# Scores by head in four 64x64 tiles, and alpha, K and Q turned by VectorE in 32x32 blocks

## The chip, the cores and the metric

The kernel runs on one core of a Trainium2 chip. The core has a matrix engine (TensorE, PE in the profile; its weight loads are listed apart, as PEld), two engines for elementwise work (VectorE, DVE, and ScalarE, ACT), a third for general work (GpSimd, POOL) and SyncE (SP), which here only issues transfers. Each engine runs its own instructions in the order in which the program gives them, and semaphores order the engines against each other. SBUF is the working memory of 128 partitions, PSUM the small memory that TensorE writes, in 8 banks of 2 KB a partition. The metric is the device time of one execution in microseconds (us), the median of several runs.

## What is computed

Two blocks follow each other. The first is a gated linear recurrence, for each of 4 batches and 8 heads over 768 steps, with states of 48x48:

```python
batch, n_heads, seq, head_dim = (4, 8, 768, 48)
for t in range(S):
    state = alpha[:, :, t, :, None] * state + np.einsum('bhd,bhe->bhde', k[:, :, t], v[:, :, t])
    y[:, :, t] = np.einsum('bhd,bhde->bhe', q[:, :, t], state)
```

Its output, as 3072 rows of 384 (8 heads x 48), goes through four experts of the second block, in f32:

```python
p = domain_probs / (domain_probs.sum(-1, keepdims=True) + 1e-09)
for e in range(E):                      # E = 4, w1: 384 x 1024, w2: 1024 x 384
    h = np.maximum(x @ w1[e], 0.0)
    out += p[:, e:e + 1] * (h @ w2[e])
```

## The kernel before, in words

**Units.** The recurrence is cut into 24 units, each one block of 128 steps of one batch, all 8 heads. `attention(u)` is a generator that emits one unit's instructions in 17 steps (numbered 0 to 16 here, by its `yield`s). Two heads share the 128 partitions: head 2p has its 48 features in rows 0 to 47 and head 2p+1 in rows 64 to 111 of pair p (rows in between are zero padding), so that a turned tensor is 128 rows x 4 pairs x 128 steps.

Steps 0, 1 and 2 bring alpha, K and Q into this form. The loaded tensors have steps on partitions (`ra`, `rk`, `rq`); `turned` (L274) turns them with four TensorE transposes into a PSUM tile, and ScalarE copies it out (AT at L288, KT at L293), or VectorE multiplies it by AT into QT (L307). Each step ends with `load(after, ...)`, which issues the load of the same tensor for a later unit into the same buffer, so that load waits until the buffer is read. `own_terms` (L296) makes the diagonal terms from `rq` and `rk` as they were loaded.

Steps 3 to 11 work through seven levels (block sizes m = 1, 2, ..., 64). For each level, `copy_q` copies the half of QT that belongs to the level to a buffer `qb`, `next_q` multiplies that half of QT by decays, and `next_k` makes the next level's KT. `copy_q` writes a block-diagonal layout: for each pair, head 2p's rows go to one column block and head 2p+1's rows to another, and the rest of `qb` stays zero (L778 sets it once). Thus one matmul of `products` (L355), with KT of a pair as weights (128 rows, 64 columns) and 64 moving columns of `qb`, gives the scores of both heads. Step 7 emits `products` of levels 0 to 3 and takes levels 0 and 1; step 8 takes 2 and 3; step 11 emits the matmuls `far` of level 6 (L410) and `products` of levels 4 and 5, and takes these. `take` is VectorE's predicated copy of scores into `near` (L365). The scores lie in PSUM tiles tagged `sc`, one bank each, two buffers, and `far` is one of them. Steps 12 and 13 copy `far` and `near` to `lat` on ScalarE (L423, L428). Then KT of the last level is turned back (`turn_keys`, L475), `result` makes the output from `lat`, V, QT and the state (`yps`, L450), and step 16 makes the new state (`sps`, L489). There TensorE uses 64-column tiles in seven units (`in_pairs`).

**Experts.** `up` (L531) makes h for one expert and a group of four units, `down` (L623) multiplies by w2 and adds up. From the second group on the operands are split into parts of fewer bits (`one` and `two` at L570, the parts of `hT` at L608, L610 and L616, with `make_dif` writing the third part). The weights are split once (`split_piece`, L228, on ScalarE and VectorE), kept in DRAM, and loaded again for each later group (L203).

**Order.** TensorE is given the experts' matmuls, and the attention steps are inserted between them: `deal` (L714) plans a due time for each step from costs per matmul, and `advance` (L763) emits a step as the planned clock passes it. The due times of neighbouring units' steps are drawn together for some pairs (`TOGETHER`), so that step 7 comes next to step 15 of the unit before and step 11 next to step 16. The order is the same in every execution. In the start, steps of units 0 and 1 are written out by hand, with `fill` matmuls that nobody reads. Nearly all loads are issued by SP, in one queue: activations (L174, L179 to L181) and weights (L203, L221, L222, L224).

Of the kernel before, what the change touches and what calls it, by code (L numbers as in the profile page):

```python
# [10 lines left out]
F32 = mybir.dt.float32  # L11
# [4 lines left out]
ALU = mybir.AluOpType  # L16
# [4 lines left out]
def kernel(  # L21
# [54 lines left out]
    HALF = P // 2  # L76
# [11 lines left out]
    ident_np = np.concatenate([np.eye(P), np.tile(np.eye(HALF), (2, 1))], 1).astype(np.float32)  # L88
# [8 lines left out]
    ident_all = const.tile([P, P + HALF], F32, name="ident")  # L97
    ident = ident_all[:, :P]
    masks = const.tile([P, 6, QUAD], U8, name="masks")
# [24 lines left out]
    early = {nm: const.tile([P, H, HD], F32, name=f"r{nm}") for nm in "akq"}  # L124
    spare = hid.tile([P, 3, 2 * NT], F32R, name="hT", bufs=NQ)
    apart = {nm: spare[:, i, :H * HD].bitcast(F32).rearrange("p (h d) -> p h d", d=HD)
             for i, nm in enumerate("akq")}
    values = [const.tile([P, H, HD], F32, name=f"rv{i}") for i in range(2)]

    blocks = [const.tile([P, NP, 2, HALF], F32, name=f"qb{i}") for i in range(4)]  # L130
    free = deque(blocks)

    def raw(u, nm):
        return values[u % 2] if nm == "v" else apart[nm] if u == 1 else early[nm]
# [32 lines left out]
    def load(u, names):  # L167
        if u >= len(units):
            return
        cb, b = units[u]  # L170
        for nm in names:
            src = srcs[nm][b, :, cb * P:(cb + 1) * P, :].rearrange("h s d -> s h d")
            if nm != "v":
                nc.sync.dma_start(out=raw(u, nm)[:, :, :D], in_=src)  # L174
                continue

            pairs = raw(u, nm).rearrange("p (a i) d -> p a i d", i=2)
            src = src.rearrange("p (a i) d -> p a i d", i=2)
# [101 lines left out]
    def attention(u):  # L280
# [7 lines left out]
        nc.scalar.copy(out=AT, in_=turned(pair(ra)))  # L288
# [3 lines left out]
        KT = keys()  # L292
        nc.scalar.copy(out=KT, in_=turned(pair(rk)))  # L293
# [13 lines left out]
        nc.vector.tensor_mul(QT, turned(pair(rq)), AT)  # L307
# [13 lines left out]
        def copy_q(li):  # L321
            m = LEVELS[li]
            qv = halves(QT, m)[:, :, :, 1, :]
            qb = free.popleft()
            qbs.append(qb)
            for i in range(2):
                rows = slice(HD * i, HD * (i + 1))
                nc.scalar.copy(out=qb[rows, :, i, :].rearrange("p a (b r) -> p a b r", r=m),  # L328
                               in_=qv[rows])
# [21 lines left out]
        def products(li, out):  # L351

            for p in range(NP):
                for s in range(2):
                    nc.tensor.matmul(  # L355
                        out[HALF * s:HALF * (s + 1), 2 * p:2 * p + 2, :],
                        lhsT=KTs[li][:, p, HALF * s:HALF * (s + 1)],
                        rhs=qbs[li][:, p, :, QUAD * s:QUAD * (s + 1)], start=True, stop=True)
            free.append(qbs[li])
# [10 lines left out]
        def scores():  # L370
            return ps.tile([P, 2, H, QUAD], F32, name="sc", tag="sc")


        for li in range(3):
# [6 lines left out]
        nc.vector.tensor_mul(near, ident_all[:, P:].unsqueeze(1).broadcast_to([P, H, HALF]),  # L381
                             dot.unsqueeze(2).broadcast_to([P, H, HALF]))
        yield
        banks = [scores() for _ in range(2)]
        for li in range(4):
            products(li, banks[li // 2][:, li % 2])
        next_q(3)
        next_k(3)
        take(0, banks[0][:, 0])
        take(1, banks[0][:, 1])  # L390
# [4 lines left out]
        take(2, banks[1][:, 0])  # L395
        take(3, banks[1][:, 1])
# [9 lines left out]
        far = ps.tile([P, NP // 2, 2, HALF], F32, name="far", tag="sc")  # L406

        for r in range(NP // 2):
            for s in range(2):
                nc.tensor.matmul(far[HALF * s:HALF * (s + 1), r],  # L410
                                 lhsT=KTs[6][:, 2 * r + s, :HALF], rhs=qbs[6][:, 2 * r + s],
                                 start=True, stop=True)
        for li in (4, 5):
            products(li, bank[:, li - 4])
        free.append(qbs[6])
        take(4, bank[:, 0])
        take(5, bank[:, 1])
        next_k(6)
        yield
        parts = lat.rearrange("p (r s i) c -> p r s i c", s=2, i=2)  # L420
        for s in range(2):
            rows = slice(HALF * s, HALF * (s + 1))
            nc.scalar.copy(out=parts[:HALF, :, s, :, HALF:], in_=far[rows])  # L423
# [12 lines left out]
        def result():  # L436
            yps = ps.tile([P, KC, P], F32, name="yps", tag="w")
            for c in range(KC):
# [9 lines left out]
                for n, (past, turn) in enumerate(turns):  # L448
                    for j, (p, i, in_v, in_st) in enumerate(turn):
# [4 lines left out]
                            rhs=QT[:, p, :] if past else lat[:, 2 * p + i, :],  # L454
# [314 lines left out]
    with tc.manual_schedule():  # L769
# [96 lines left out]
```

## Time and profile before

| | |
|---|---|
| median of 3 runs | 1053.27 us (1052.65 to 1053.30) |
| span of the profiled execution, first to last instruction | 1050.8 us |
| granted TensorE clock, mean | 1.000 |
| TensorE matmuls | 1033.8 us busy, 98%, 8554 instructions |
| TensorE weight loads | 899.2 us busy, 86% |
| VectorE | 778.3 us busy, 74% |
| ScalarE | 565.7 us busy, 54% |
| GpSimd | 37.7 us busy, 4% |
| DMA, mean of 16 engines | 69%, 251.66 MB, 158549 packets |

The span is what the profiler saw of one execution; the runs' times include 2 to 3 us around it. The busy times are sums over an engine's instructions, with overlaps counted once. A busy TensorE is not one at its peak, since its matmuls are pipelined and their ends are modelled; starts are measured. The attention of all units ends at about 836 us, and the last 200 us are experts alone.

The profile also has, for the instructions of the change (count, busy us, mean ns): TensorE's transposes of ra, rk and rq 92 each, about 14 us each; L355 2304 matmuls, 77.2 us; L410 192, 15.5 us; ScalarE's copies AT and KT (L288, L293) 24 each, 14.0 us each; VectorE's QT (L307) 24, 16.4 us, 685.

### The profile page before, as it was taken

What the parts mean: (1) busy time and instruction counts of PE and PEld (TensorE: products, weight loads), DVE (VectorE), ACT (ScalarE), POOL (GpSimd) and SP (SyncE); (2) the same over time, 40 slices, a digit from 0 to 9 for tenths busy, and PEclk for the clock granted to TensorE, in tenths of its full rate; (3) what the DMA queues carried; (4) which work ended last, traced back from release to release, by engine and by line L of the source; (5) the groups of instructions that cost most, each with busy time, mean ns of one, the idle gap of its engine ahead of it and who ended that gap; (6) DMA issues with size and microseconds to landing.
All of it is one profiled execution on the core that took longest, in us unless ns stands there. A gap on an engine that the chain in (4) does not pass through costs nothing.

```text
span 1050.8 us, 21723 instructions
## 1 busy us (share of the span) xinstructions
PE 1033.8 (98%) x8554; PEld 899.2 (86%) x8554; DVE 778.3 (74%) x1620; ACT 565.7 (54%) x1195; POOL 37.7 (4%) x81
## 2 busy tenths in 40 slices
PE   8899999999999999999999999999999999999998
PEld 8777777687787899898898998898989989898998
DVE  5588777668779868778877777987887875656565
ACT  4687876575657545447456436565474453323232
POOL 3000010000001000000000000000000000000000
PEclk9999999999999999999999999999999999999999
DMA  7596699997868949669669569577594454444531
GB/s 118 161 333 210 241 313 352 320 344 235 300 247 260 382 154 317 270 210 303 241 214 336 187 219 366 183 271 258 170 361 179 183 211 180 182 184 177 207 154 46
DMA packets 158549, 251.66 MB, mean 239 GB/s; under 512 B 120144, under 2 KB 134864, under 8 KB 135920
## 3 DMA queue, kind: packets, MB, share of 16 engines
q1 hardware_dynamic: 151984, 207.89, 58.7%
q0 software_dynamic: 6016, 42.08, 10.0%
q8 instruction: 67, 1.10, 0.4%
q10 hardware_dynamic: 448, 0.32, 0.1%
q14 instruction: 34, 0.28, 0.1%
HBM read 207.79 MB, written 42.47 MB: 238 GB/s over the span
## 4 chain that ended last, share of the span: by engine, by line
PE 85%; DVE 5%; ACT 4%; DMA 2%; issue 2%; SPq 1%; POOL 0%; ACTq 0%; DVEq 0%; POOLq 0%
PE ops L663 36%; PE one L570 23%; PE two L570 11%; PE sc L355 6%; PE yps L450 3%; PE tp L277 3%; ACT qb L328 2%; PE one L562 1%; PE sps L489 1%; DMA hT<-in_moe_w_dram 1%; PE far L410 1%; DVE hT L616 1%; DMA w<-in_moe_w_dram 1%; DVE near L365 1%; DVE QT L335 1%
## 5 line engine op out<-in xcount | busy, mean ns | idle before, releaser
L663 PE MATMUL ops<-w,hT 128*128 128x384 f32 x1872 | 342.7, 340 | 0.2 <-DVE hT L616 0.2
L663 PEld LDWEIGHTS ops<-w,hT 128*128 128x128 f32 x1872 | 322.6, 188 | 4.0 <-ACT t L581 0.6
L570 PE MATMUL one<-xT,w 128*128 128x512 f32 x960 | 251.8, 398 | 0.4 <-ACT t L581 0.4
L570 PEld LDWEIGHTS one<-xT,w 128*128 128x128 f32 x960 | 176.1, 188 | 38.3 <-ACT t L581 1.2
L581 ACT ACTIVATE t<-one 128x512 f32<-128x512 f32 (+1 forms) x192 | 106.7, 556 | 175.1 <-PE one L570 169.9
L328 ACT COPY qb<-QT 64x256 f32<-64x256 f32 x336 | 136.6, 407 | 58.2 <-DVE QT L335 30.3
L610 DVE SCALAR_TENSOR_TENSOR hT<-t,hT 128x512 fp32r<-128x512 f32 (+1 forms) x172 | 110.4, 642 | 63.3 <-ACT hT L608 62.0
L583 DVE TENSOR_TENSOR t<-t,two 128x512 f32<-128x512 f32 (+1 forms) x172 | 109.2, 635 | 53.2 <-PE two L570 32.0
L608 ACT ACTIVATE hT<-t 128x512 fp32r<-128x512 f32 (+1 forms) x172 | 101.8, 592 | 86.8 <-DVE t L583 86.2
L570 PE MATMUL two<-xT,w 128*128 128x512 f32 x480 | 136.5, 393 | 0.1
L570 PEld LDWEIGHTS two<-xT,w 128*128 128x128 f32 x480 | 90.0, 188 | 20.5 <-DVE acc L692 0.9
L663 PE MATMUL ops<-hT 128*128 128x384 f32 x288 | 100.8, 492 | 0.6 <-DMA hT<-in_moe_w_dram 0.3
L616 DVE SCALAR_TENSOR_TENSOR hT<-hT 128x512 fp32r<-128x512 f32 (+1 forms) x172 | 100.6, 634 | 0.0
L365 DVE COPY_PREDICATED near<-masks,sc 128x256 f32<-128x256 uint8 x144 | 77.0, 535 | 22.2 <-PE sc L355 19.3
L335 DVE TENSOR_TENSOR QT<-QT,dec 128x256 f32<-128x256 f32 x144 | 61.0, 423 | 38.8 <-ACT qb L328 38.3
L355 PEld LDWEIGHTS sc<-qb,KT 128*64 128x64 f32 x2304 | 72.7, 138 | 9.0 <-issue 4.4
L355 PE MATMUL sc<-qb,KT 128*64 128x64 f32 x2304 | 77.2, 223 | 2.6 <-ACT qb L328 2.6
L663 PEld LDWEIGHTS ops<-hT 128*128 128x128 f32 x288 | 52.1, 190 | 30.6 <-DMA hT<-in_moe_w_dram 1.2
L692 DVE SCALAR_TENSOR_TENSOR acc<-ops,p_all,acc 128x384 f32<-128x384 f32 x82 | 49.8, 614 | 27.2 <-PE ops L663 26.3
L347 ACT COPY KT<-KT 128x256 f32<-128x256 f32 x138 | 57.5, 417 | 5.1 <-PE sc L355 1.9
L348 DVE TENSOR_TENSOR KT<-KT,dec 128x256 f32<-128x256 f32 x144 | 60.0, 417 | 0.0
L562 PE MATMUL one<-xT,w 128*128 128x256 f32 (+1 forms) x240 | 46.7, 341 | 0.6 <-ACT xT L467 0.6
(90 smaller groups left out, 932.4 us busy)
## 6 DMA issues: line engine op xcount, KB each, us to landing
w<-kept SPq DMA_DIRECT2D x144, 1152.0 KB
kept<-w POOLq DMA_DIRECT2D x32, 1152.0 KB, 7.3
hT<-in_moe_w_dram SPq DMA_DIRECT2D x32, 384.0 KB
w<-in_moe_w_dram SPq DMA_DIRECT2D x48, 128.0 KB
ra<-in_alpha_dram SPq DMA_DIRECT2D x23, 192.0 KB
rk<-in_k_dram SPq DMA_DIRECT2D x23, 192.0 KB
rq<-in_q_dram SPq DMA_DIRECT2D x23, 192.0 KB
out_dram<-acc POOLq DMA_DIRECT2D x22, 192.0 KB, 7.0
```

The source lines that it names most:

```text
L328: nc.scalar.copy(out=qb[rows, :, i, :].rearrange("p a (b r) -> p a b r", r=m), in_=qv[rows])
L335: nc.vector.tensor_mul(qv, qv, spread(dv[:, :, :, 0], m))
L348: nc.vector.tensor_mul(new[:, :, :, 0, :], old[:, :, :, 0, :], spread(halved(decs[li])[:, :, :, 1], m))
L355: nc.tensor.matmul(out[HALF * s:HALF * (s + 1), 2 * p:2 * p + 2, :], lhsT=KTs[li][:, p, HALF * s:HALF * (s + 1)], rhs=qbs[li][:, p, :, QUA ...
L365: nc.vector.copy_predicated(near.rearrange("p a (b two r) -> p a b two r", two=2, r=m)[:, :, :, 1, :], mk.unsqueeze(1).broadcast_to([P, H, ...
L570: nc.tensor.matmul(out, lhsT=w[:, part, kc], rhs=x_part(gi, part, kc), start=(part == terms[0] and kc == 0), stop=(part == terms[-1] and k ...
L581: nc.scalar.activation(out=t, in_=one, func=ACT.Copy, scale=FINE)
L583: nc.vector.tensor_add(t, t, two)
L608: nc.scalar.activation(out=top, in_=x, func=ACT.Relu, scale=TRIM)
L610: nc.vector.scalar_tensor_tensor(out=low, in0=x, scalar=0.0, in1=top.bitcast(F32), op0=ALU.max, op1=ALU.subtract)
L616: nc.vector.scalar_tensor_tensor(out=dif, in0=top.bitcast(F32), scalar=1 / 4096.0, in1=low.bitcast(F32), op0=ALU.mult, op1=ALU.subtract)
L663: nc.tensor.matmul(sums[at], lhsT=h, rhs=w, start=(n == begins[at]), stop=(n == ends[at]))
```

## The change

1. **Loads.** Units 0 and 1 keep the old loads, now both in the spare `hT` buffer (`early[u]`). For all later units alpha, K and Q are also, or instead, loaded into `runs_of`: partition 32g+t, for quadrant g (head parity i = g // 2, and features 0 to 31 or from 32 on by g % 2), holds the four steps 4t to 4t+3 of each of the four heads of that parity, as one contiguous run of 176 elements (160 for the second kind). That is four loads a tensor. K and Q are loaded in the old form too, for `own_terms`, without padding; alpha is not.
2. **Turning.** `turn` is one VectorE transpose of 32x32 blocks over the whole tile, into AT, KT or QT in place of `turned` and the copies. The padding rows 48 to 63 then hold other steps' features instead of zeros; QT is multiplied by a column `features` (1 for rows of real features, 0 for others) along with AT.
3. **Scores by head.** `copy_q` is one ScalarE copy, and `qb` is half as large with no zeros in it. `products` and `far` make one matmul per head and column half, of 64 rows and 64 weight columns, with 32 (`far`: 64) moving columns, so that four tiles of 64x64 of the array are used. Heads are ordered by parity in `near`, `lat` and the scores.
4. **PSUM.** The scores of four levels lie in one tile of two banks, one bank for each row half, with a single buffer; `far` is a part of it.

```diff
-    ident_np = np.concatenate([np.eye(P), np.tile(np.eye(HALF), (2, 1))], 1).astype(np.float32)
+    ident_np = np.concatenate([np.eye(P), np.tile(np.eye(HALF), (2, 1)),
+                               np.arange(P)[:, None] % HD < D], 1).astype(np.float32)
...
-    early = {nm: const.tile([P, H, HD], F32, name=f"r{nm}") for nm in "akq"}
     spare = hid.tile([P, 3, 2 * NT], F32R, name="hT", bufs=NQ)
-    apart = {nm: spare[:, i, :H * HD].bitcast(F32).rearrange("p (h d) -> p h d", d=HD)
-             for i, nm in enumerate("akq")}
+    early = [{nm: spare[:, i, u * H * HD:(u + 1) * H * HD].bitcast(F32).rearrange("p (h d) -> p h d", d=HD)
+              for i, nm in enumerate("akq")} for u in range(2)]
+    rows_of = {nm: const.tile([P, H, D], F32, name=f"r{nm}") for nm in "kq"}
+    NTOK = P // QUAD
+    RUN = (NTOK - 1) * D + QUAD
+    runs_of = {nm: const.tile([P, NP, RUN], F32, name=f"s{nm}") for nm in "akq"}
...
-    blocks = [const.tile([P, NP, 2, HALF], F32, name=f"qb{i}") for i in range(4)]
+    blocks = [const.tile([P, NP, HALF], F32, name=f"qb{i}") for i in range(4)]
...
-                nc.sync.dma_start(out=raw(u, nm)[:, :, :D], in_=src)
+                for g in range(P // QUAD if u >= 2 else 0):
+                    i, tail = divmod(g, 2)
+                    off, n = (QUAD, RUN - HD // 4) if tail else (0, RUN)
+                    runs = srcs[nm][b].rearrange("(a i) s d -> i a (s d)", i=2)[
+                        i, :, cb * P * D:(cb + 1) * P * D].rearrange("a (t n) -> t a n", t=QUAD)
+                    nc.sync.dma_start(out=runs_of[nm][QUAD * g:QUAD * (g + 1), :, :n],
+                                      in_=runs[:, :, off:off + n])
+                if u < 2 or nm != "a":
+                    nc.sync.dma_start(out=raw(u, nm)[:, :, :D], in_=src)
...
-        nc.scalar.copy(out=AT, in_=turned(pair(ra)))
+        def turn(nm, out):
+            t = runs_of[nm]
+            t = bass.AP(tensor=t.tensor, offset=t.offset, ap=[list(t.ap[0]), [RUN, NP], [D, NTOK], [1, QUAD]])
+            nc.vector.transpose(out=out.rearrange("p a (t n) -> p a n t", n=NTOK), in_=t)
+        if u < 2:
+            nc.scalar.copy(out=AT, in_=turned(pair(ra)))
+        else:
+            turn("a", AT)
...
-        nc.scalar.copy(out=KT, in_=turned(pair(rk)))
+        if u < 2:
+            nc.scalar.copy(out=KT, in_=turned(pair(rk)))
+        else:
+            turn("k", KT)
...
-        nc.vector.tensor_mul(QT, turned(pair(rq)), AT)
+        if u < 2:
+            nc.vector.tensor_mul(QT, turned(pair(rq)), AT)
+        else:
+            turn("q", QT)
+            nc.vector.scalar_tensor_tensor(out=QT, in0=QT, scalar=features, in1=AT,
+                                           op0=ALU.mult, op1=ALU.mult)
...
-            for i in range(2):
-                rows = slice(HD * i, HD * (i + 1))
-                nc.scalar.copy(out=qb[rows, :, i, :].rearrange("p a (b r) -> p a b r", r=m),
-                               in_=qv[rows])
+            nc.scalar.copy(out=qb.rearrange("p a (b r) -> p a b r", r=m), in_=qv)
...
             for p in range(NP):
-                for s in range(2):
-                    nc.tensor.matmul(
-                        out[HALF * s:HALF * (s + 1), 2 * p:2 * p + 2, :],
-                        lhsT=KTs[li][:, p, HALF * s:HALF * (s + 1)],
-                        rhs=qbs[li][:, p, :, QUAD * s:QUAD * (s + 1)], start=True, stop=True)
+                for i in range(2):
+                    rows = slice(HD * i, HD * (i + 1))
+                    for s in range(2):
+                        nc.tensor.matmul(
+                            out[HALF * s:HALF * (s + 1), NP * i + p, :],
+                            lhsT=KTs[li][rows, p, HALF * s:HALF * (s + 1)],
+                            rhs=qbs[li][rows, p, QUAD * s:QUAD * (s + 1)], start=True, stop=True)
...
-            return ps.tile([P, 2, H, QUAD], F32, name="sc", tag="sc")
+            return ps.tile([P, H, P], F32, name="sc", bufs=1)
+        level = lambda t, j: t[:, :, QUAD * j:QUAD * (j + 1)]
...
-        far = ps.tile([P, NP // 2, 2, HALF], F32, name="far", tag="sc")
+        far = bank[:, :, HALF:]
         for r in range(NP // 2):
-            for s in range(2):
-                nc.tensor.matmul(far[HALF * s:HALF * (s + 1), r],
-                                 lhsT=KTs[6][:, 2 * r + s, :HALF], rhs=qbs[6][:, 2 * r + s],
-                                 start=True, stop=True)
+            for i in range(2):
+                rows = slice(HD * i, HD * (i + 1))
+                for s in range(2):
+                    nc.tensor.matmul(far[HALF * s:HALF * (s + 1), NP * i + 2 * r + s, :],
+                                     lhsT=KTs[6][rows, 2 * r + s, :HALF],
+                                     rhs=qbs[6][rows, 2 * r + s], start=True, stop=True)
...
-        for nm in "akq":
-            for r in (early[nm], apart[nm]):
-                nc.gpsimd.memset(r[:, :, D:], 0.0)
+        for r in (early[u][nm] for u in range(2) for nm in "akq"):
+            nc.gpsimd.memset(r[:, :, D:], 0.0)
         nc.gpsimd.memset(lat[HALF:, :, :HALF], 0.0)
-        for t in values + blocks:
+        for t in values:
             nc.gpsimd.memset(t, 0.0)
         for t in sts[:-1]:
             nc.gpsimd.memset(t, 0.0)
+        for t in runs_of.values():
+            nc.gpsimd.memset(t[:, :, RUN - HD // 4:], 0.0)
```

`products` is called with `level(bank, li)` for levels 0 to 3 and `level(bank, li - 4)` for levels 4 and 5, and `take` likewise; `result` reads `lat[:, NP * i + p, :]`. The schedule's costs, due times and beats are as before.

More of the change, by code (lines that the diff above doesn't have):

```diff
@@ L95 @@
     ps = ctx.enter_context(tc.tile_pool(name="ps", bufs=2, space=bass.MemoryType.PSUM))
-    ident_all = const.tile([P, P + HALF], F32, name="ident")
+    ident_all = const.tile([P, P + HALF + 1], F32, name="ident")
     ident = ident_all[:, :P]
+    diagonal = ident_all[:, P:P + HALF]
+    features = ident_all[:, P + HALF:]
     masks = const.tile([P, 6, QUAD], U8, name="masks")
@@ L121 @@
     srcs = {"a": alpha, "k": k, "q": q, "v": v}
-    early = {nm: const.tile([P, H, HD], F32, name=f"r{nm}") for nm in "akq"}
     spare = hid.tile([P, 3, 2 * NT], F32R, name="hT", bufs=NQ)
-    apart = {nm: spare[:, i, :H * HD].bitcast(F32).rearrange("p (h d) -> p h d", d=HD)
-             for i, nm in enumerate("akq")}
+    early = [{nm: spare[:, i, u * H * HD:(u + 1) * H * HD].bitcast(F32).rearrange("p (h d) -> p h d", d=HD)
[4 more added lines that the diff above has]
+    runs_of = {nm: const.tile([P, NP, RUN], F32, name=f"s{nm}") for nm in "akq"}
     values = [const.tile([P, H, HD], F32, name=f"rv{i}") for i in range(2)]
-    blocks = [const.tile([P, NP, 2, HALF], F32, name=f"qb{i}") for i in range(4)]
+    blocks = [const.tile([P, NP, HALF], F32, name=f"qb{i}") for i in range(4)]
     free = deque(blocks)
     def raw(u, nm):
-        return values[u % 2] if nm == "v" else apart[nm] if u == 1 else early[nm]
+        return values[u % 2] if nm == "v" else early[u][nm] if u < 2 else rows_of.get(nm)
     xTs = {}
@@ L379, in attention @@
         copy_q(3)
-        nc.vector.tensor_mul(near, ident_all[:, P:].unsqueeze(1).broadcast_to([P, H, HALF]),
-                             dot.unsqueeze(2).broadcast_to([P, H, HALF]))
+        nc.vector.tensor_mul(
+            near.rearrange("p (i a) n -> p i a n", i=2),
+            diagonal.unsqueeze(1).unsqueeze(1).broadcast_to([P, 2, NP, HALF]),
+            dot.rearrange("p (a i) -> p i a", i=2).unsqueeze(3).broadcast_to([P, 2, NP, HALF]))
         yield
-        banks = [scores() for _ in range(2)]
+        bank = scores()
         for li in range(4):
-            products(li, banks[li // 2][:, li % 2])
+            products(li, level(bank, li))
         next_q(3)
         next_k(3)
-        take(0, banks[0][:, 0])
-        take(1, banks[0][:, 1])
+        take(0, level(bank, 0))
+        take(1, level(bank, 1))
         yield
@@ L394, in attention @@
         next_k(4)
-        take(2, banks[1][:, 0])
-        take(3, banks[1][:, 1])
+        take(2, level(bank, 2))
+        take(3, level(bank, 3))
         yield
@@ L405, in attention @@
         bank = scores()
-        far = ps.tile([P, NP // 2, 2, HALF], F32, name="far", tag="sc")
+        far = bank[:, :, HALF:]
         for r in range(NP // 2):
-            for s in range(2):
-                nc.tensor.matmul(far[HALF * s:HALF * (s + 1), r],
-                                 lhsT=KTs[6][:, 2 * r + s, :HALF], rhs=qbs[6][:, 2 * r + s],
-                                 start=True, stop=True)
+            for i in range(2):
[4 more added lines that the diff above has]
+                                     rhs=qbs[6][rows, 2 * r + s], start=True, stop=True)
         for li in (4, 5):
-            products(li, bank[:, li - 4])
+            products(li, level(bank, li - 4))
         free.append(qbs[6])
-        take(4, bank[:, 0])
-        take(5, bank[:, 1])
+        take(4, level(bank, 0))
+        take(5, level(bank, 1))
         next_k(6)
         yield
-        parts = lat.rearrange("p (r s i) c -> p r s i c", s=2, i=2)
+        by_half = lambda t: t.rearrange("p (i r s) c -> p s i r c", i=2, s=2)
         for s in range(2):
             rows = slice(HALF * s, HALF * (s + 1))
-            nc.scalar.copy(out=parts[:HALF, :, s, :, HALF:], in_=far[rows])
+            nc.scalar.copy(out=by_half(lat)[:HALF, s, :, :, HALF:], in_=by_half(bank)[rows, s, :, :, HALF:])
         yield
@@ L453, in result @@
                             else flat_v[:, p, in_v:in_v + QUAD],
-                            rhs=QT[:, p, :] if past else lat[:, 2 * p + i, :],
+                            rhs=QT[:, p, :] if past else lat[:, NP * i + p, :],
                             start=(n == 0), stop=(n == len(turns) - 1))
```

## The prediction

> **What bounds the kernel.** I read the chain of waits first, then the busy time by stretch, the waits of TensorE, the pieces of the chain around single units, and the groups of instructions.
>
> ```profile
> PE 85%; DVE 5%; ACT 4%; DMA 2%; issue 2%; SPq 1%; POOL 0%; ACTq 0%; DVEq 0%; POOLq 0%
> ```
>
> ```profile
> 50.00:836.00 786.00, 778.49 (x6802) 663.67 (x6802) 617.78 (x1289) 467.56 (x986) 24.69 (x46) 1.00 0.77 267
> 25.00:150.00 125.00, 116.07 (x1195) 92.10 (x1196) 90.46 (x206) 94.89 (x217) 7.05 (x13) 1.00 0.78 243
> ```
>
> In the second view the columns are stretch, length, busy time of PE, weight loads, VectorE, ScalarE and GpSimd, granted clock, DMA share, GB/s. TensorE sets the end. From 25 to 150 us it loses 8.9 us; from 175 us on its list of waits holds two, 0.6 us together. VectorE is idle for 168 us of the 786 in which the 22 later units run: 7.6 us a unit. So a TensorE microsecond removed after 150 us comes off the end, if nothing else becomes late.
>
> ```profile
> PE yps L450 <- ACT lat L428: 2.8, 3, 1.4
> PE sc L355 <- ACT qb L328: 2.6, 3, 1.2
> PE far L410 <- DVE t L298: 1.3, 1, 1.3
> ...
> PE far L410 <- ACT qb L328: 0.8, 1, 0.8
> ```
>
> These are total, times and longest wait, in us. The early losses hang on ScalarE's copies.
>
> What one unit's work costs TensorE shows in the chain's pieces (start, length, line, number of matmuls), from one late and one early unit:
>
> ```profile
> 426.97 2.02 PE sc L355 x64
> ...
> 442.26 0.60 PE sps L489 x16
> 442.87 0.45 PE far L410 x8
> 443.32 0.93 PE sc L355 x32
> ...
> 446.53 0.44 PE tp L277 x4
> ...
> 449.05 0.44 PE tp L277 x4
> ```
>
> ```profile
> 84.52 0.86 PE sps L489 x8
> ```
>
> A plain f32 matmul is two passes, each a weight load and a matmul. The reader should compare three rows. At L355 a level's 16 pairs (64 weight columns, 64 moving columns, two column tiles) take 0.465 us: single starts come in twos, 7 ns apart, every 58 ns. At L489 in 64-column tiles only 48 columns move, and the rhythm is the same 58 ns. At L489 with 128-column weights and 96 moving columns it is 111 ns (0.86 us for 8), although 128-column weights with 128 moving take about as long at L562 (112 ns). So the **weight load** sets the rhythm, by its columns (111/128 and 58/64 are nearly the same per column), not the moving rows. Only at `far` (128 moving, 64 weight columns) does the moving side set it: twos every 109 ns.
>
> **The change, part by part.**
>
> *Turning by TensorE goes* for a, K and Q of 22 units. Each turn is a 0.44 us piece between matmuls: 22 x 3 x 0.44 = **-29.0 us**. Where a turn follows a 64-column piece it lasts 0.58; the difference is the change of tile mode, which the next matmul then pays.
>
> *Products of levels 0 to 5.* 8 matmuls of 128 rows become 16 of 64 rows, so 32 pairs instead of 16, but over four tiles instead of two. The weights keep 64 columns. If the four loads run beside each other, 8 rounds of 58 ns remain: 0.465 us, **0**. No row has row tiles. Bound below: if half the rows load in half the time, 0.23 us less for each of 24 x 6 levels, -34 us. Bound above: if the two row halves take turns, or pairs cannot follow faster than the mean 29 ns of L355, 32 x 29 = 0.93 us, 144 x 0.465 = +67 us. I take 0: the nearest row is L450, where four column tiles of one round start 7 ns apart without disturbing each other.
>
> [...]
>
> *`far`.* 64 moving columns instead of 128, and four tiles: 16 pairs in 4 rounds of 58 = 0.23 for 0.45: 24 x 0.21 = **-5 us** (0 if the row halves take turns).
>
> *Tile modes.* In 7 units `sps` in 64-column tiles stands right before `far`; the modes now differ. A change costs 0.15 us between starts (L355 to L570 at 444 us): **+1 us** (0 to +3).
>
> *ScalarE.*
>
> ```profile
> L328 ACT COPY qb<-QT 64x256 f32<-64x256 f32 x336 | 136.6, 407 | 58.2 <-DVE QT L335 30.3
> L347 ACT COPY KT<-KT 128x256 f32<-128x256 f32 x138 | 57.5, 417 | 5.1 <-PE sc L355 1.9
> ```
>
> Two half copies of 0.407 become one of the shape of L347, 0.417: 168 x 0.40 = 67 us less, and 22 x 2 copies of 0.583 (L288, L293) go, 26 us. ScalarE is not the bound, so this counts only in the early losses: of the 8.9 us, 4 hang on qb copies or turned tiles. **-4 us** (-8 to 0).
>
> *VectorE* gets 66 transposes of 128x512. No row shows one. From below L428's VectorE copy of 64x512, 0.42 us; from above L365, 0.535 for 256 elements, 1.07 for 512. I take 0.69, the 512-element two-input rows: 2.1 us a unit, 46 us in all. The masked multiply for QT (as L610, 0.64) replaces one of 0.685. The cover is the 7.6 us of idle time a unit. What becomes late is `dif` at L616: around 410 to 419 us VectorE never rests, its last L616 ends 1.8 us before TensorE needs it, TensorE now comes 0.9 us sooner and VectorE has up to 1.4 us more ahead of it. Some 0.4 us in a third of the units: **+3 us** (0 to +12).
>
> [...]
>
> *Transfers.* For a later unit three loads of 1024 runs of 192 B become twelve quadrant loads (128 runs of 704 or 640 B each) and two of the old kind, 0.59 to 1.44 MB. The added bytes at about 400 GB/s are 2.1 us of all engines a unit. At 405 to 416 us a unit's loads fall at the end of a burst, followed by an idle stretch, and are used 35 us later: nothing there. SP has 11 more issues, 0.4 us each. Behind them in its queue stand the next `rv` and weight loads. In the early part no slack hides it: SP issues ra, rk and rq of unit 2 at 24.1 to 30.3, then v, then the second expert's weights, and a piece of the chain is `41.68 7.24 DMA w<-in_moe_w_dram`, just ahead of the work that waits for it. Fourteen issues for three: +1 to +6 there, and the same kind of piece ends at 153 us (0 to +5): **+5 us** (0 to +11). The load of the next a now waits for VectorE's turn instead of TensorE's, within a microsecond of the old time; the weights behind it have over 6 us.
>
> *Nothing moves* from one score bank instead of two: the levels of steps 7 and 11 are taken before the next use, as `take` stands at steps 7, 8 and 11. Layout by head is only addresses; `take`, `near` and `result` keep their sizes.
>
> Sum: -29 + 0 - 5 + 1 - 4 + 3 + 5 = **-29 us**. From the profiled span of 1050.8 that is 1021.8; the median of the runs is 2.5 above the span: **1024 us**.
>
> **The rivals.** *Row halves take turns in loading weights*, or pairs issue no faster than before: levels at 0.93 us and no gain at `far`. For it: no four-tile rhythm faster than 27 ns a pair is in the trace; against: tiles at L450 and L355 overlap freely. +67 + 5 gives **1096**, slower. It decides from a level of 0.465 + 29/144 = 0.67 us; half of it gives **1060**.
>
> *VectorE becomes the bound.* For it: 79% busy from 50 to 836 us, and the strided write of the turn has no row. At 2.6 us a transpose VectorE's 618 us become 790, 35 more than the 755 that TensorE would need: **1059**; below about 2.1 us it doesn't decide.
>
> *The gain is given back*, the transposes being off TensorE but weights or `dif` late instead. For it: a 0.2 us wait on L616 and the two DMA pieces; against: two waits in 875 us. Half of the removed 38: **1043**.
>
> *Smaller tiles load faster*: -27 more, **997**.
>
> **How the numbers follow.** Forecast 60% (own range 1010 to 1038), turns in full 13%, in part 9%, VectorE 6%, given back 8%, faster loads 4%. A difference under 0.2% (2 us) can't be told from none. Faster: 60 + 8 + 4 and 2 of the part case, 74%; same 3% (part case); slower 13 + 4 + 6 = 23%. The range goes from 1005, the favourable bounds of the small terms, to 1067, past VectorE and the part case with their margins; left out are the full turns, the faster loads and some tails, 20%.
>
> **What would show it.** Right: 128 products in a piece of about 2.0 us and 16 `far` pairs in about 0.25; turns at x8 a tensor for L277's ra, rk and rq; matmuls 8554 + 2304 + 192 - 264 = 10786; 66 transposes near 0.7 us; 168 qb copies near 0.42; PE waits after 175 us of a few us. Wrong: products of 3 us or more, TensorE waiting for VectorE or for `w`, a DMA piece before 60 us grown by more than 6 us.

## The result, and the profile after

The changed kernel takes **1111.01 us** (median of 4 runs, 1109.55 to 1112.23), beside 1052.96 of the kernel before on the same chip: 1.055 times as long (95% interval 1.0528 to 1.0568). The forecast was 1024, faster; time and sign are wrong.

The same views as before, first the chain of waits and the busy time by stretch (stretch, length, busy PE, weight loads, VectorE, ScalarE, GpSimd, granted clock, DMA share, GB/s):

```profile
PE 59%; DVE 20%; DMA 9%; issue 5%; SPq 5%; ACT 1%; DVEq 0%; POOL 0%; ACTq 0%; POOLq 0%
```

```profile
50.00:836.00 786.00, 734.09 (x8292) 609.93 (x8293) 636.91 (x1267) 360.86 (x753) 24.77 (x46) 0.97 0.82 273
25.00:150.00 125.00, 105.84 (x1541) 81.11 (x1542) 93.69 (x203) 64.46 (x153) 5.48 (x10) 0.89 0.76 233
```

TensorE no longer sets the end alone (59% of the chain, 85 before), and the clock is no longer 1.00. Over the whole span TensorE is idle for 71.5 us (17.0 before) and busy for 1037.0 (1033.8), at a mean clock of 0.971. If the 2.9% that the clock lacks of 1108.5 us fell on busy time, that is 32 us, and the work itself is 1005 us at full clock: some 29 us less than before, near the 33 forecast for TensorE's own rows (-29, -5 and +1). By this estimate most of what was forecast to go did go. The question is where 54 us of waits and 32 of slow clock come from.

TensorE's waits (total us, times, longest):

```profile
PE ops L701 <- DVE hT L654: 12.5, 18, 3.1
PE sc L387 <- issue: 11.4, 5, 3.6
PE ops L701 <- DMA hT<-in_moe_w_dram: 7.6, 3, 3.7
PE one L608 <- DVE acc L730: 5.1, 2, 4.8
PE tp L293 <- DVE KT L377: 5.1, 3, 4.1
```

Three causes stand here: VectorE late with `dif` (L654, before at L616), weights late (`hT`), and, in the middle of a row of products (L387, before at L355), waits for nothing that the profile shows ("issue").

Pieces of the chain around one late unit (start, us, what):

```profile
411.37 1.89 DVE hT L654 x3
...
416.80 2.87 PE ops L701 x15
419.67 1.67 PE yps L488 x56
421.33 2.00 PE sc L387 x128
423.33 1.94 PE ops L701 x10
425.27 1.38 PE one L608 x6
```

The 128 products take 2.00 us, as 64 did (2.02). Ahead of them VectorE's `dif` is on the chain, in the very stretch in which before it ended 1.8 us early.

The groups that the change made (count, then busy us and mean ns of one, then idle time before):

```profile
L307 DVE STREAM_TRANSPOSE AT<-sa 128x512 f32<-128x512 f32 x22 | 24.4, 1110 | 0.0
...
L338 DVE SCALAR_TENSOR_TENSOR QT<-QT,ident,AT 128x512 f32<-128x512 f32 x22 | 16.5, 751 | 0.8
...
L358 ACT COPY qb<-QT 128x256 f32<-128x256 f32 x168 | 68.4, 408 | 154.1 <-DVE QT L338 77.2
```

The transposes are the surprise: 1.10 us each where 0.69 was taken. The copies are as forecast (0.408, forecast 0.417).

The "issue" waits can be seen whole in one place. Pieces of the chain around 555 us, and below them the busy time by stretch (columns as above; the last but two is the clock):

```profile
553.13 1.64 PE sc L387 x102
554.77 3.65 issue
558.41 1.06 PE sc L387 x26
559.47 2.86 PE one L608 x6
```

```profile
545.00:554.00 9.00, 8.79 (x148) 6.72 (x149) 8.39 (x18) 1.81 (x5) 2.16 (x4) 1.00 0.60 209
...
559.00:563.00 4.00, 4.00 (x23) 3.16 (x20) 1.97 (x3) 0.63 (x2) 0.00 (x0) 0.50 0.02 5
563.00:567.00 4.00, 4.00 (x18) 3.32 (x17) 3.35 (x9) 2.39 (x6) 0.00 (x0) 0.97 0.63 214
```

A row of 128 products stops after 102 for 3.65 us, with no semaphore to wait for. After the gap six matmuls of L608 take 2.86 us, where at 425 us they took 1.38: the clock is at 0.50 until about 563.3 us, and then back. So a gap is paid for twice.

### The profile page after: what moved, and what is told of

Its sections match the earlier page's. It is cut to its first block, busy times and chain, and to the rows that moved or that the text cites. A ratio compares the mean times of both kernels' runs of the same rounds, so it can differ in the third digit from the quotient of the medians.

```text
span 1108.5 us, 26353 instructions
## 1 busy us (share of the span) xinstructions
PE 1037.0 (94%) x10786; PEld 888.4 (80%) x10786; DVE 838.9 (76%) x1686; ACT 468.7 (42%) x983; POOL 36.3 (3%) x80
## 4 chain that ended last, share of the span: by engine, by line
PE 59%; DVE 20%; DMA 9%; issue 5%; SPq 5%; ACT 1%; DVEq 0%; POOL 0%; ACTq 0%; POOLq 0%
PE ops L701 23%; PE one L608 18%; PE two L608 9%; PE sc L387 4%; DVE hT L654 4%; DMA sa<-in_alpha_dram 3%; PE yps L488 3%; DMA w<-kept 2%; SPq L237 2%; DMA w<-in_moe_w_dram 1%; DVE QT L364 1%; DVE near L397 1%; DVE acc L730 1%; DVE t L621 1%; DVE QT L307 1%
## 5 line engine op out<-in xcount | busy, mean ns | idle before, releaser
L701 PE MATMUL ops<-w,hT 128*128 128x384 f32 x1872 | 346.9, 342 | 17.9 <-DVE hT L654 12.5
L701 PEld LDWEIGHTS ops<-w,hT 128*128 128x128 f32 x1872 | 326.5, 190 | 29.9 <-DVE hT L654 18.8
L608 PE MATMUL one<-xT,w 128*128 128x512 f32 x960 | 256.3, 403 | 7.6 <-DVE acc L730 5.1
L608 PEld LDWEIGHTS one<-xT,w 128*128 128x128 f32 x960 | 180.8, 192 | 48.5 <-DVE acc L730 6.5
L648 DVE SCALAR_TENSOR_TENSOR hT<-t,hT 128x512 fp32r<-128x512 f32 (+1 forms) x172 | 110.2, 641 | 54.7 <-ACT hT L646 54.1
L608 PE MATMUL two<-xT,w 128*128 128x512 f32 x480 | 138.1, 397 | 0.1
L358 ACT COPY qb<-QT 128x256 f32<-128x256 f32 x168 | 68.4, 408 | 154.1 <-DVE QT L338 77.2
L701 PE MATMUL ops<-hT 128*128 128x384 f32 x288 | 105.1, 515 | 9.0 <-DMA hT<-in_moe_w_dram 7.6
L608 PEld LDWEIGHTS two<-xT,w 128*128 128x128 f32 x480 | 91.3, 191 | 21.2 <-DVE acc L730 1.2
L654 DVE SCALAR_TENSOR_TENSOR hT<-hT 128x512 fp32r<-128x512 f32 (+1 forms) x172 | 100.8, 635 | 0.0
L387 PE MATMUL sc<-qb,KT 64*64 64x32 f32 x4608 | 82.0, 224 | 16.0 <-issue 11.4
L387 PEld LDWEIGHTS sc<-qb,KT 64*64 64x64 f32 x4608 | 77.2, 141 | 23.0 <-issue 17.1
L701 PEld LDWEIGHTS ops<-hT 128*128 128x128 f32 x288 | 55.0, 198 | 44.7 <-issue 5.9
L364 DVE TENSOR_TENSOR QT<-QT,dec 128x256 f32<-128x256 f32 x144 | 60.8, 422 | 20.5 <-ACT qb L358 19.8
L600 PE MATMUL one<-xT,w 128*128 128x256 f32 (+1 forms) x240 | 49.0, 359 | 2.7 <-DVE acc L730 1.9
```

Of the source, the lines that this page charges most:

```text
L358: nc.scalar.copy(out=qb.rearrange("p a (b r) -> p a b r", r=m), in_=qv)
L364: nc.vector.tensor_mul(qv, qv, spread(dv[:, :, :, 0], m))
L387: nc.tensor.matmul(out[HALF * s:HALF * (s + 1), NP * i + p, :], lhsT=KTs[li][rows, p, HALF * s:HALF * (s + 1)], rhs=qbs[li][rows, p, QUAD ...
L608: nc.tensor.matmul(out, lhsT=w[:, part, kc], rhs=x_part(gi, part, kc), start=(part == terms[0] and kc == 0), stop=(part == terms[-1] and k ...
L648: nc.vector.scalar_tensor_tensor(out=low, in0=x, scalar=0.0, in1=top.bitcast(F32), op0=ALU.max, op1=ALU.subtract)
L654: nc.vector.scalar_tensor_tensor(out=dif, in0=top.bitcast(F32), scalar=1 / 4096.0, in1=low.bitcast(F32), op0=ALU.mult, op1=ALU.subtract)
```

## The experiments

Theory after the result, with four causes: (A) TensorE's long rows outrun their instructions; (B) VectorE's longer work makes `dif` late; (C) the quadrant loads make weights and activations late; (D) each such gap brings half clock behind it. Its rival: the products by head themselves (four tiles) or the tile modes are dearer than they look, and the waits only follow from that.

### The parts of the change, one by one

`heads_only` has the scores by head alone; loads and turning are those of before:

```diff
-        if u < 2:
-            nc.scalar.copy(out=AT, in_=turned(pair(ra)))
-        else:
-            turn("a", AT)
+        nc.scalar.copy(out=AT, in_=turned(pair(ra)))
...
```

> The kernel before with the scores by head alone (64x64 tiles, one ScalarE copy per level); a, K and Q are loaded and turned by TensorE as before. Theory A (the loss comes from the turns: VectorE three times 1.10 us a unit, and the quadrant loads): this kernel is a little faster than before, by 24 x 0.14 us at far and some of the early losses, 1046 to 1050 us, with TensorE idle below 12 us and the clock near 1.0. Theory B (the loss comes from TensorE's instruction stream: 128 pairs in 1.85 us outrun the fetch, each stall is 3 to 4 us and is followed by about 7 us of half clock): slower than before, 1065 to 1085 us, with stalls in the middle of a row of score products that no semaphore explains.

Measured: 1065.0, ratio 1.0129 (1.0112 to 1.0145). Its list of TensorE's waits has the stalls, and its clock is 0.994:

```profile
PE sc L358 <- issue: 7.8, 5, 3.2
```

`load_once` keeps everything but issues the quadrant loads for unit 2 alone, `act_copy` keeps the loads and lets ScalarE copy in place of VectorE's transposes, and `load_once_act_copy` does both:

```diff
-                for g in range(P // QUAD if u >= 2 else 0):
+                for g in range(P // QUAD if u == 2 else 0):
```

```diff
-            nc.vector.transpose(out=out.rearrange("p a (t n) -> p a n t", n=NTOK), in_=t)
+            nc.scalar.copy(out=out.rearrange("p a (t n) -> p a n t", n=NTOK), in_=t)
```

> The changed kernel, but the quadrant loads are issued for unit 2 alone; the later units turn the same data again, so the output is of wrong a, K and Q. VectorE's transposes, the scores by head and the old loads of K and Q stay. Theory A1 (VectorE's time is what makes TensorE wait): within 10 us of the changed kernel's 1111. Theory A2 (the twelve loads and their place in SP's queue make weights and q late): 1060 to 1080 us. Theory B: 1095 to 1111, the stalls in the score products stay.

> The changed kernel, but ScalarE copies the loaded runs into AT, KT and QT where VectorE turned them (same addresses, not turned, so the output is wrong); the quadrant loads stay and wait for these copies. VectorE has 66 x 1.10 = 73 us less. Theory A1: back below the kernel before, 1020 to 1040 us. Theory A2: within 15 us of 1111. Theory B: 1060 to 1085.

> Both: loads for unit 2 alone and ScalarE copies in place of the turns, so the output is of wrong data. TensorE's order is that of the changed kernel. If instructions and the score bank cost nothing, TensorE's saving of 33 us is all that is left: 1015 to 1025 us. Under theory B 1045 to 1070, with the stalls in the score products.

Measured: 1091.32, 1091.87 and 1064.71 (ratios 1.0374, 1.0382 and 1.0125). Without its loads the change costs 20 us less, without VectorE's transposes 19 less, without both 46 less. Neither of the first two falls into the range of a theory with one cause, and the stalls stay in all three (11.4 to 11.8 us at L387). So three causes lie side by side, and the third belongs to the scores by head. That `load_once_act_copy` ends where `heads_only` does is chance: its TensorE makes 66 turns less, but is idle for 41.3 us against 28.4, at a clock of 0.980 against 0.994.

`far_only` takes only the `far` matmuls by head into the kernel before, with the scores in one tile of two banks as in the change.

> The kernel before, with only the last level's products (far) by head in 64x64 tiles, levels 0 to 5 as before. The rhythm of 58 ns for 64 weight columns then gives 16 pairs in 0.24 us where 8 took 0.385: 24 x 0.14 = 3.4 us off, 1048 to 1050; no long row of instructions is made, so no stalls. If the gain of far is eaten by changes of tile mode in the seven units where sps stands before it, and by the next level's: 1051 to 1053.

Measured: 1053.28 (12 runs), ratio 1.0004 (0.9995 to 1.0014). Nothing is gained, and the single buffer for the scores costs nothing. `far` and the products behind it as pieces of the chain, first here, then in `heads_split` (below), where both are by head:

```profile
442.60 0.39 PE sc L418 x16
443.00 1.08 PE sc L359 x32
```

```profile
664.69 0.39 PE sc L421 x16
665.08 0.91 PE sc L358 x64
```

The kernel before has 0.45 and 0.93 at 442.87 us. In `far_only` the products keep their two tiles, so the tile mode changes between the two rows, and what `far` gains is lost behind it. With both rows by head no change stands between them. By starts, from the first of `far` to the first behind the products, it takes 1.52 us before (1.48 in the seven units with `sps` in front), 1.47 in `far_only`, and 1.30 in `heads_split` and, where nothing waits, in the changed kernel. In those seven units `far` now starts 0.15 us after the last of `sps`, in place of 0.05. So the changed kernel has the gain at `far`, though `far_only` has not.

### A: the long rows

`heads_split` is `heads_only` with the products of levels 0 and 1 emitted one step earlier, so that a row has 64 pairs and not 128; `after_split` is the same edit on the changed kernel:

```diff
+        bank = scores()
+        for li in range(2):
+            products(li, level(bank, li))
...
         yield
-        bank = scores()
-        for li in range(4):
+        for li in range(2, 4):
```

> The kernel with the scores by head alone (1065.0), but the products of levels 0 and 1 are issued one step earlier than those of levels 2 and 3, so that 64 pairs stand at a place instead of 128; same instructions, up to 24 more changes of tile mode in and out (0.3 us each, 7 us at most). Theory B (the fetch of TensorE's instructions is outrun by 128 pairs in 1.85 us): the stalls inside L358 go, with the half clock behind them; 1050 to 1060 us. If the stalls come from something else at the score bank or the row tiles: 1065 to 1075, stalls as before.

> The changed kernel with the same split of its products. Theory B, whose share in the changed kernel I put at 11 us of stalls and half of that again as half clock: 1111 falls to 1095 to 1105. If the stalls aren't a matter of the length of the row: 1110 to 1120.

Measured: 1052.37 against 1052.68 (10 runs, ratio 1.000, 0.9991 to 1.0009) and 1092.49, 18.5 less than the changed kernel. Neither has a wait at "issue" of more than 0.3 us any more. So the stalls are due to the length of the row: its 128 products are 128 weight loads and 128 matmuls in 1.85 us. The queue that the profile's page calls q8, instruction, has one packet of 16,384 B for about 254 of TensorE's instructions (85 packets beside 21,572 instructions; before 67 beside 17,108), and at 554.77, 836.39 and 873.92 us such a packet starts 0.9 to 1.3 us into the stall, while the row goes on 1.3 to 1.5 us after it has landed. All seven of the changed kernel's waits at "issue" of over 0.4 us, four of them outside these three stalls, have such a packet start between 1.7 us before them and 1.3 us into them. That the packet is what the row waits for is read from these times; that a shorter row removes the stall is shown. Also, `heads_split` speaks against the rival: with the stalls gone, the products by head cost no more in all than before. Its gain of 0.22 us a unit at `far` goes into the second place for products: from first start to what follows, two rows of 64 take 1.07 us each, where one row took 2.02 before.

### B: VectorE

`split_early_dif` is `after_split` with `make_dif` emitted every 5 matmuls in place of every 7, so that VectorE gets to it sooner:

```diff
-            if later and n % (len(steps) // 12 - 1) == len(steps) // 12 - 2:
+            if later and n % max(1, len(steps) // 16 - 1) == max(1, len(steps) // 16 - 1) - 1:
```

> The changed kernel with the split products (1092.5), and make_dif issued after every fifth matmul of a full down instead of every seventh, so that VectorE's last dif stands 16 matmuls (2.8 us) earlier in its order. Theory A1 in a sharper form (VectorE is late at one place, the dif that TensorE needs in the last third of down, 12.3 us of waits on L656 and the half clock behind the longest): 1075 to 1085, the waits on dif below 4 us. If VectorE is late everywhere: 1088 to 1096, the waits only change their line.

Measured: 1083.55, 9 us less than `after_split`. The wait for `dif`, first in `after_split`, then here:

```profile
PE ops L703 <- DVE hT L656: 12.3, 17, 3.1
```

```profile
PE ops L703 <- DVE acc L732: 7.7, 6, 2.9
...
PE ops L703 <- DVE hT L656: 2.6, 8, 0.9
```

Now VectorE's `acc` is what comes late. An order written for a shorter VectorE can be mended in part; the work remains.

`flat_turn` lets the transpose write its blocks one after the other, in place of with a stride of four elements (the tensors are then in another order):

```diff
-            nc.vector.transpose(out=out.rearrange("p a (t n) -> p a n t", n=NTOK), in_=t)
+            nc.vector.transpose(out=out.rearrange("p a (n t) -> p a n t", n=NTOK), in_=t)
```

> The changed kernel, with the turned blocks written as contiguous runs of 32 elements where the change writes every fourth element, so that the steps stand in another order and the output is wrong. If the stride of the writes makes a transpose 1.10 us, it falls to 0.55 to 0.7 us and the run to 1090 to 1100; if a 4-byte transpose has that pace by itself, 1.05 to 1.10 and 1106 to 1115.

Measured, in one run: 1099.12. One of its three groups:

```profile
L307 DVE STREAM_TRANSPOSE QT<-sq 128x512 f32<-128x512 f32 x22 | 15.5, 704 | 0.0
```

The forecast's 0.69 happens to be the price of a contiguous write; the stride costs 0.40 us a transpose, 66 x 0.40 = 26 us of VectorE, and by this single run some 12 us of the end.

`after_pool` lets GpSimd make `dif`, in two instructions.

> The changed kernel, but the third part of h (make_dif, 172 x 0.635 us = 101 us of VectorE) is made by GpSimd in two instructions. Theory A1 (TensorE waits because VectorE has too much ahead of dif, acc and K): the waits on L654, 12.5 us, and part of the others go; 1085 to 1098. If VectorE's own chain of the levels is what is late, and not its load: 1105 to 1115.

Measured: 1146.12. GpSimd needs 1514 + 1278 ns for a `dif` for which VectorE needs 635, TensorE now waits 16.4 us for GpSimd, and VectorE's L648 goes from 641 to 805 ns beside it. The test says nothing about B.

### C: the loads

`after_late` issues the loads of a, K and Q, in both forms, three steps later, so that SP's queue does not stand before a buffer that VectorE still reads (55.6 us of SP's waits for the turn of alpha in the changed kernel).

> The changed kernel, but the loads of the next unit's a, K and Q are issued three steps later (with levels 0, 1 and 2), when VectorE has long turned this unit's. All bytes and descriptors stay; only SP's waiting for VectorE goes. If the loads cost time because SP waits for the turns and the weights stand behind it: 1085 to 1098. If they cost by their number and bytes: 1108 to 1115.

Measured: 1121.75, worse, and the expectation was wrong. That wait fell to 22.7 us, but what was loaded late landed late (the waits of VectorE, then of TensorE):

```profile
DVE t L325 <- DMA rq<-in_q_dram: 21.8, 2, 18.2
```

```profile
PE two L609 <- ACT t L620: 14.8, 2, 14.1
```

The edit trades SP's waiting for late data, so it shows that data which land late cost, and not what SP's waiting costs by itself. Three kernels on the base of `split_early_dif` size this. `sed_no_load` has no quadrant loads, with constants in the buffers, and VectorE turns these; in `sed_none` ScalarE copies the constants and nothing turns them; `sed_act_queue` issues the quadrant loads on ScalarE's queue, three steps later:

```diff
-                for g in range(P // QUAD if u >= 2 else 0):
+                for g in range(0):
...
```

> The same kernel with VectorE's turns kept (of constants, so the output is wrong) and no quadrant load. If the loads are what is left of the loss: 1040 to 1055. If VectorE still holds TensorE up with dif early: 1060 to 1070.

> The changed kernel with split products and early dif (1083.6), without any quadrant load and with ScalarE copies of constants in place of VectorE's turns, so the output is of wrong a, K and Q. The three causes (instruction fetch, VectorE's 73 us, the loads) are then all taken away. If they are all there is: the saving of TensorE is left, less 24 more changes of tile mode (7 us at most), 1020 to 1032. If 1040 or more: something in the scores by head or the order is still unexplained.

> The changed kernel with split products and early dif (1083.6), the quadrant loads issued from ScalarE's queue, three steps later, so that nothing in SP's queue stands behind them or behind the turns; same bytes and descriptors. If the loads cost by standing ahead of the weights in SP's queue: 1060 to 1072. If by their bytes and number, or by landing late: 1080 to 1095.

Measured: 1059.37, 1038.64 and 1160.74. The loads cost 24.2 us (1083.55 to 1059.37), VectorE's turning 20.7 more; the 1038.64 lie between the two ranges expected. ScalarE's queue, used like this, is no way out (1160.74 lies far outside both ranges; GpSimd's queue was not tried): the chain of `sed_act_queue` has weights that now take 12 us to land, and its ScalarE holds up VectorE (90 us of waits at L364):

```profile
105.16 12.31 DMA w<-in_moe_w_dram
```

Where along the span each share falls is seen in the start of one and the same matmul in each kernel, the 241st, 1801st and last of the experts' second product (single starts of the trace, us):

| kernel | 241st | 1801st | between | last |
|---|---|---|---|---|
| before | 245.7 | 923.8 | 678.1 | 1046.4 |
| after | 277.4 | 981.2 | 703.8 | 1103.9 |
| `split_early_dif` | 272.6 | 952.8 | 680.2 | 1075.7 |
| `sed_no_load` | 250.0 | 931.4 | 681.4 | 1054.1 |
| `sed_none` | 243.0 | 907.5 | 664.5 | 1030.2 |
| `heads_split` | 244.9 | 923.4 | 678.5 | 1046.1 |
| `late_turn_start` (below) | 245.6 | 918.0 | 672.4 | 1040.7 |

The loads cost 22.6 us up to the 241st and nothing behind it (680.2 and 681.4). VectorE's turns cost 16.9 us between the 241st and the 1801st (681.4 and 664.5); TensorE's gaps there are 10.2 us longer and half clock takes some 1.7 us more; the other 5 stay open.

The beginning shows how the loads do it. SP's queue, before and after (start, us, line, what), and what TensorE waits for, after:

```profile
24.09 0.95 SPq L174 DMA_DIRECT2D ra<-in_alpha_dram  x1
...
30.37 2.17 SPq L224 DMA_DIRECT2D hT<-in_moe_w_dram  x4
```

```profile
23.31 3.40 SPq L187 DMA_DIRECT2D sa<-in_alpha_dram  x4
...
33.96 2.77 SPq L240 DMA_DIRECT2D hT<-in_moe_w_dram  x4
...
38.23 2.29 PE L701 MATMUL ops<-hT 128*128 128x384 f32 x3 [3.67 <-DMA hT<-in_moe_w_dram]
```

The weights stand behind fourteen issues in place of three, leave 3.6 us later, and TensorE waits 3.67 us for them.

### A version that is faster than both

From these shares: keep the split rows, turn on VectorE only where loads have slack (from unit 10 on), and only two of the three tensors (alpha and K), so that VectorE keeps room. That is `late_turn`; `heads_split_dif` is the same without turning, to part the turns from the earlier `dif`.

```diff
-        nc.scalar.copy(out=AT, in_=turned(pair(ra)))
+        if u < TURN:
+            nc.scalar.copy(out=AT, in_=turned(pair(ra)))
+        else:
+            turn("a", AT)
...
```

> The kernel with the scores by head and the split (1052.4), with VectorE turning only a and K, and only from unit 10 on, and dif early as above. Q is turned by TensorE for all units, so no mask is needed; the first ten units are loaded and turned as before. If the turn pays wherever VectorE has 2.2 us to spare and no transfer is tight: 14 x 2 x 0.44 = 12 us off, 1038 to 1044. If VectorE's lateness eats it even there: 1050 to 1060.

> The kernel with the scores by head and the split (1052.4) with dif early, and no turn by VectorE: the partner of late_turn (1049.3). If the turn of a and K from unit 10 on is what gains there: 1051 to 1054. If early dif gains by itself: 1048 to 1050.

Measured: 1049.32 (10 runs), ratio 0.9968 (0.9958 to 0.9979), and 1052.66, ratio 1.000 (0.999 to 1.001): the gain is the turns'. It is half of the 12 us expected: between the 241st and the 1801st matmul `late_turn` gains 6.1 us on `heads_split`, and its TensorE has 4.5 us of gaps there, nearly all for VectorE, where `heads_split` has none. `late_turn` lost 3 to 4 us at its start, where SP's first load waited for the clearing of the alpha buffer. `late_turn_start` clears only what that load doesn't write, and `late_turn_6` also starts turning at unit 6:

```diff
-        nc.gpsimd.memset(runs_of["a"], 0.0)
+        nc.gpsimd.memset(runs_of["a"].rearrange("p a n -> p (a n)")[:, H * HD:], 0.0)
```

> late_turn with one edit: only the part of the alpha buffer that the first unit's load does not write is set to zero, so that SP's first load no longer waits for the whole clearing. In late_turn SP's first load is issued at 3.98 us of the span, in heads_split at 0.74. Theory (the 3 to 4 us by which late_turn is behind heads_split at its first matmul of the experts' second product, 38.0 against 33.9 us, are this wait alone, and TensorE keeps what it gains later): first load at about 0.74 us, 1045 to 1047 us, 0.993 to 0.995 of the kernel before. Rival (the lead is used up by a later wait, for the first weights or for unit 1's rq): 1048 to 1050.

> late_turn_start, with VectorE turning alpha and K from unit 6 on instead of 10 (18 units instead of 14). Theory (from some 250 us on each pair of turns taken off TensorE is worth what units 10 to 23 gain, 5.7 us for 14 units by the starts of the same matmuls, 0.4 us a unit): 1.6 us less than late_turn_start, 1043.5 to 1046. Rival (units 6 to 9 fall in the stretch before 260 us in which loads and weights have no slack, and what the quadrant loads delay there is given back, with half clock): as much as late_turn_start or up to 10 us more.

Measured: **1046.82** against 1052.55, ratio 0.9946 (0.9933 to 0.9958), which is 5.7 us below the kernel before; and 1056.52, ratio 1.0041, 9.7 us more for four units more. A load of `late_turn_6` that lands late (TensorE's waits):

```profile
PE tp L293 <- DMA rq<-in_q_dram: 9.8, 2, 8.7
```

Up to the 241st matmul it is 7.3 us behind `late_turn_start`, at the last 8.1. The same turns pay from unit 10 on and lose before, where the old-form load of Q, issued behind the new ones and the weights, comes 8.7 us late.

## Why the prediction was wrong, step by step

Two terms of the sum were mis-sized, VectorE's (+3) and the transfers' (+5); the stalls in the doubled rows and the half clock were put at nothing; and the gain of turning was counted where TensorE waits anyway. Medians share the distance out, in the order in which the edits were made (in another order the shares differ: without the loads alone 20, without VectorE's transposes alone 19): from 1111.0 the split rows take 18.5, the earlier `dif` 9.0, no quadrant loads 24.2, no turns on VectorE 20.7; 1038.6 remain, 15 above the forecast.

- *Turning, -29.0*: right as work, too large as a gain. `sed_none`, in which copies on ScalarE stand for all 66 turns, is 13.7 below `heads_split` (it also loads no alpha, so it is a bound and not a version). Between the 241st and 1801st matmul it gains 14.0, where the trace of before has 42 of the 66 turns (18.5 at 0.44); 2.8 of the difference are new gaps. The other 24 lie in the first 246 us, forecast 10.6, and gain 1.9: TensorE's gaps there grow by 4.8 us, and half clock takes some 3.4 more. The prediction itself read that a microsecond removed after 150 us comes off the end, and then counted all 22 units.
- *Products, 0*: the rhythm was right. 128 products take 1849 ns from first to last start (64 before: 1864), 14.5 ns a pair, so the row halves don't take turns, and pairs follow closer than the 27 ns of L450 that spoke for the rival. (A product is one pass: the 1152 f32 matmuls that the program gives at L355 are 2304 matmuls and 2304 weight loads in the trace of before.) The step failed in what it left out: twice the instructions in the same time. That cost 18.5 us with its half clock, and none of the rivals had it.
- *`far`, -5, and tile modes, +1*: right as work. 16 starts lie within 243 ns; `far` and the products behind it together take 0.22 us less in 17 units and 0.18 in the seven with `sps` in front, where the change of mode adds 0.10: 4.3 us in all for the -4 forecast. `far_only`, where the products keep their tiles, has no such gain.
- *VectorE, +3*: mis-sized, the main failure beside the loads. The transpose takes 1.10 and not 0.69, the masked multiply 0.751 and not 0.64; and 3.3 + 0.1 us a unit inside a cover of 7.6 idle us a unit cost 20.7, and 9.0 more until `dif` stood earlier. The idle time is an average; `dif` and `acc` fall due in stretches in which VectorE has none. The rival "VectorE becomes the bound" said that below 2.1 us a transpose doesn't decide, and was wrong for the same reason.
- *Transfers, +5*: mis-sized, 24.2. The place was right (the beginning, weights behind fourteen issues), the size was not: it was priced from two pieces of the chain, +1 to +6 and 0 to +5, and by the 241st matmul 22.6 us were lost. There the traces of `split_early_dif` and `sed_no_load` differ by 14.3 us of TensorE's gaps and, by the granted clock, some 10 us of half clock, which the price left out.
- *ScalarE, -4*: the copies are as forecast. In `heads_split`, which has the halved copies but keeps those of AT and KT, TensorE's waits for ScalarE in the whole run fall from 8.9 to 5.5 us, but 3.3 us of waits for the load of `rq` appear, and the 241st matmul comes 0.8 us sooner. In the changed kernel the early losses grew by other waits, so the term can't be told there.
- *The missing step*: half clock. Of the changed kernel's 14 gaps of TensorE of 1.81 us or more after 20 us, 13 are followed by a clock of 0.50 to 0.64 in the next 4 us; of the nine gaps between 0.9 and 1.77 us none. In all kernels of this case taken together, counted in the same way, 120 of 130 gaps of 1.8 us or more are followed by a clock below 0.9. No sharp limit shows: in the changed kernel a gap of 2.35 us (at 466.96) leaves the clock at 1.00 and one of 1.81 (at 250.48) is followed by 0.57, and in `heads_split` a gap of 2.27 us leaves it at 1.00 and one of 1.76 is followed by 0.68. The kernel before had no gap over 1.45 us, so its trace could not show it.
- *Rivals*: "the gain is given back" named the right things, late weights and late `dif`, and priced them at half the gain. They came to more than all of it.

## What to carry to other kernels

Work taken off the bounding engine is worth its time only in the stretches where that engine is never waiting, so count it by stretch, and do the same for the cover on the engine that takes the work over: its average idle time is no cover for work that falls due at once. Doubling the number of tiny instructions in one row (here to 256 in 1.85 us) needs a look at whether the row runs through, not only at how fast its instructions run. Where an edit pays in one part of the span and loses in another, as the turns from unit 10 on and before, make it in the one part only.

## What was unexpected of the hardware

- A row of 256 TensorE instructions in 1.85 us can stop for 3.4 to 3.7 us in its middle with no semaphore (three of the changed kernel's 24 such rows); rows of half that length did not.
- Most gaps of TensorE from 1.8 us on are followed by half clock (13 of 14 in the changed kernel); no sharp limit shows (2.35 us left the clock at 1.00, 1.81 was followed by 0.57).
- The tile mode counts between rows: `far` by head gains 0.22 us a unit when the products behind it use the same tiles (`heads_split`, 1.52 to 1.30), and nothing to speak of when they don't (`far_only`, 1.47).
- A VectorE transpose of 32x32 blocks of 128x512 f32 took 0.70 us with a contiguous write (`flat_turn`), 1.10 with a stride of 16 B (the changed kernel).
- With GpSimd at work on f32 tiles beside it (`after_pool`), VectorE's L648 took 805 ns on the mean; in the changed kernel 641.
